# TensorE in the program's order through layer 1, W' made by pairs, and memory work one turn a step

## The chip, the cores and the metric

The kernel runs on one core of a Trainium2 chip. The metric is the device time of one execution in microseconds, as the median of several runs.

## The reference

Attention with a memory of 32 slots is followed by two MoE layers, each a product, a nonlinearity and a product. With B = 4, H = 8, S = 576, D = 64, M = 32 there are 2304 tokens of width 512; the hidden width is 2048.

```python
def _attn_ref(q, k, v, phi):            # per batch and head
    a = softmax(phi, over=s)
    k_m = einsum('bhsm,bhsd->bhmd', a, k)
    v_m = einsum('bhsm,bhsd->bhmd', a, v)
    attn = softmax(q @ k_m.T / sqrt(D), over=m)
    return attn @ v_m

def _moe_ref(x, w_in, w_out):
    h = np.maximum(x @ w_in, 0.0)
    return h * h @ w_out

def _moe2_ref(x, w_in, w_out):
    h = x @ w_in
    g = h * tanh(log1p(exp(h)))
    return g @ w_out
```

The output is `_moe2_ref(_moe_ref(attention))`.

## The kernel before

**Layer 1.** The product of the attention's `v_m` with `w_in` is made first, per batch and per page of 256 hidden columns. The result is W', called `wp` in the code: the first layer is then attention weights (128 rows: four heads times 32 slots, two groups of heads) times W'. `w_part` (line 580) makes one W' part (b, j) for batch b and page j: 8 small matmuls in the program, 16 in the trace, into a PSUM tile with the tag "bb" of two banks. `w_pair` (line 605) makes two, (b, j) and (b, j + 1), 16 in the program and 32 in the trace. In both, ScalarE (ACT) then casts the sum to the high half and VectorE (DVE) subtracts for the low half; in `w_pair` the two halves of the tile are taken one after the other, either at once or, by `w_out`, in the next step. There is one buffer of "bb", and three others use it: the scores (`psc`, line 536), the transposes of softmaxed phi (`pt`, line 464), and the W' parts. A block there waits until the block ahead has been read out.

**A step.** `a_tile` (line 724) runs over hidden blocks fc of 128. A step makes `h` by six matmuls for each segment of tokens (lines 713 to 715, the first product), then ACT applies relu and square, copies to `g` (line 742), and DVE subtracts for the low half of `g` (line 745). The second product, 12 matmuls of `a` from `g` (lines 665 to 667), is put LAG = 3 steps behind. `tick` starts weight work on ACT, DVE and the queues, `mid` a piece of the attention of a later batch, `post` the W' work. Banks of `h` are "mm" and "b0" in turns, or "mm" alone.

**The tiles.** `subs` holds four narrow tiles (b = 0, 1 and both halves of 288 tokens) for hidden blocks 0 to 3, then two passes of three wide tiles of 344, 464 (232 of batch 0 and 232 of batch 1) and 344 tokens, for blocks 4 to 9 and 10 to 15. Behind these come four narrow tiles, both halves of batch 2 and of batch 3, with all 16 blocks each, and then the second layer. Batches 2 and 3 get their memory products meanwhile: `kv_later` returns a generator of turns (`kv_unit`, line 515), `attn_later` one for scores and softmax; `run_step` takes so many turns a step. A turn of `kv_unit` uses "b0" for `pk` (the product of softmaxed phi with k and v) and `pkt` (its transpose), and loads phi, k and v of the next batch on SP's queue.

**The weights of layer 2** are folded at the same time: `raw_i` and `raw_o` are loaded on SP's queue, ACT and DVE make the sums and casts `st` in tiles that share space with the outputs `ys`, POOL's queue stores them, and layer 1's outputs are stored to `y` on SP's queue (line 698).

**What sets the order.** Instructions go through a list scheduler that arranges each engine's order by a simulated timeline; it may put a block of W' earlier or cut it. Within `written(...)` the engines named keep the program's order: the first tile on DVE and ACT, and the second layer on TensorE, DVE and ACT. Everything between was free before. Steps (fc) below are counted from 0 in each tile.

Of the kernel before, what the change touches and what calls it, by code (L numbers as in the profile page):

```python
# [8 lines left out]
F32R = mybir.dt.float32r  # L9
# [7 lines left out]
B, H, S, D, M = 4, 8, 576, 64, 32  # L17
DM, FF = 512, 2048
P = 128
# [21 lines left out]
def body(tc, q, kvm, kvt, phi, w_in1, w_out1, w_in2, w_out2, out):  # L41
# [21 lines left out]
    def page(shape, dt, name):  # L63
        return PG.tile(shape, dt, tag="pg", name=name, bufs=NPG)
# [8 lines left out]
    for p in range(2):  # L73
        t = Y.tile([P, (NC + 1) * P], F32, name=f"phi{p}")
# [62 lines left out]
    wt = {}  # L137
# [15 lines left out]
    @contextlib.contextmanager  # L153
    def written(*engines):

        traced = nc.cur_bb.bb.instructions
        last = {x.engine: x for x in traced}
        seen = traced[-1]
        yield
        start = next(k for k in reversed(range(len(traced))) if traced[k] is seen) + 1  # L160
        for x in traced[start:]:
            if x.engine not in engines:
                continue
            if x.engine in last:
                tc.add_manual_dep(
                    x, last[x.engine].name,
                    mybir.DependencyInfo(mybir.DependencyClass.NoSync, mybir.DependencyReason.DATA),
                    reason="written")
            last[x.engine] = x
# [265 lines left out]
    rc_t, et_t, kk_t, kT, vT = {}, {}, {}, {}, {}  # L435
# [142 lines left out]
    wp = {}  # L578

    def w_part(b, j, lo, hi, split=False):  # L580

        ps = banks2(f"pw{b}{j}{lo}")[:, :, :hi - lo]
        for g in range(4):
            for p in range(2):
                nc.tensor.matmul(  # L585
                    ps[M * g:M * g + M, p], vT[b][D * p:D * p + D, M * g:M * g + M],
                    wt["i1", j][D * p:D * p + D, g, lo:hi], start=True, stop=True)
        if (b, j) not in wp:
            wp[b, j] = page([P, 2, 2, 256], F32R, f"wp{b}{j}")
        t = wp[b, j]  # L590
        nc.scalar.copy(t[:, 0, :, lo:hi], ps)
        rest = lambda: nc.vector.tensor_sub(t[:, 1, :, lo:hi], ps, t[:, 0, :, lo:hi].bitcast(F32))
        if split:
            return rest
        rest()
# [6 lines left out]
                f()  # L602
        wait_w.clear()

    def w_pair(b, j, now=False):

        ps = banks2(f"pw{b}{j}p")
        for i in range(2):
            for g in range(4):
                for p in range(2):  # L610
                    nc.tensor.matmul(
                        ps[M * g:M * g + M, p, 256 * i:256 * i + 256],
                        vT[b][D * p:D * p + D, M * g:M * g + M],
                        wt["i1", j + i][D * p:D * p + D, g], start=True, stop=True)

        def take(i):
            t = wp[b, j + i] = page([P, 2, 2, 256], F32R, f"wp{b}{j + i}")
            nc.scalar.copy(t[:, 0], ps[:, :, 256 * i:256 * i + 256])
            nc.vector.tensor_sub(t[:, 1], ps[:, :, 256 * i:256 * i + 256], t[:, 0].bitcast(F32))

        for i in range(2):
            if now:
                take(i)
            else:
                wait_w.append(lambda i=i: take(i))
# [131 lines left out]
    bounds = [sum(GROUPS[:i]) for i in range(len(GROUPS) + 1)]  # L757
# [13 lines left out]
    def place(i):  # L771
        if i in deep:
# [3 lines left out]
    c1 = Conv(order, place,  # L776
              lambda key, u: key != "i1" or u < 8 or (1, u // 2 - 4) in wp)
# [244 lines left out]
    def kv_later(b):  # L1022
        def nxt(p):
            if p == 0 and b > 1:
                load_kv(b, 1)
            if b + 1 < B:
                load_phi(b + 1, p)
                if p == 1:
                    load_kv(b + 1, 0)
                    load_tail(b + 1)  # L1030
        u = lazy(lambda: kv_unit(b, "b0", nxt))

        return [[u, 3], [iter(range(2)), 2], [u, 4]] if b > 1 else [[u, 5]]

    def attn_later(b, half):
        def nxt():
            if b < 2:
                if (b, half) == (1, 0):
                    load_q(2, 0)
                return  # L1040
            nb, nh = (b, 1) if half == 0 else (b + 1, 0)
            if nb < B:
                load_q(nb, nh)
        return [[lazy(lambda: attn_unit(b, half, nxt)), 5 if b > 1 else 4]]
# [3 lines left out]
    subs = [(0, bounds[1], half_of(b, half)) for b in range(2) for half in range(2)]  # L1048
# [14 lines left out]
    lanes, n_steps = [], 1  # L1063
    for i, (f0, f1, segs) in enumerate(subs):
        b, half, part = i // 2, i % 2, (i - 4) % 3 if i > 3 else None
        final = i == len(subs) - 1
        if i == 0:
            with written(mybir.EngineType.DVE, mybir.EngineType.Activation):
                first_tile()
            c1.hold = False  # L1070
            c1.store()
            c1.load(2 * GROUPS[0] - 3)
            continue
        elif i == 1:
            c1.limit, c1.after, c1.paced = 2 * GROUPS[0], "lo", True
            lanes, n_steps = [[iter(range(2)), 2]] + attn_later(1, 1), 1
        elif i == 2:
            c1.limit, c1.after = len(c1.order), (1, 0)
        elif i == 3:
            drain(lanes)  # L1080
            c1.after = (1, 1)
            load_q(2, 0)
            load_phi(2, 0)
            load_phi(2, 1)
            load_kv(2, 0)
            load_tail(2)
        elif i == 4:
            c1.after = None
        elif i == len(subs) - 2:
            lanes, n_steps = kv_later(2), 2  # L1090
        elif final:
            drain(lanes)
            lanes, n_steps = attn_later(2, 0), 2
            load_page(0)
            load_page(1)

        def tick(fc):
            if len(c1.done) < 2 * NF:
                c1.tick()
            else:  # L1100
                if not fold.loaded:
                    fold.load(3)
                if part and fc - f0 in (0, LAG + 1):
                    fold.tags = (("x", "at"), ("ys0", "x", "at"), ("ys0",), ("ys0", "ys1"))[
                        2 * part - 2 + (fc > f0)]
                if final or part == 1 and fc > f0:
                    fold.tick(pops=1)

        def mid(fc):
            run_step(lanes, n_steps)  # L1110

        def post(fc):
            if part is None:
                if half == 0 and fc % 2 == 0 and fc + 2 < f1 and i != 2:
                    c1.need("i1", fc + 3)
                    w_part(b, fc // 2 + 1, 0, 256)
                if i == 1 and fc + 1 == f1:
                    w_part(1, fc // 2, 0, 256)
                if half == 1 and fc + 2 == f1:
                    if b == 0:  # L1120
                        w_part(1, f0 // 2, 0, 256)
                    else:
                        c1.need("i1", f1 + 1)
                        w_part(0, f1 // 2, 0, 256)
            elif part == 0:
                if (fc - f0) % 2 == 0 and fc + 2 < f1:
                    c1.need("i1", fc + 3)
                    w_part(0, fc // 2 + 1, 0, 256)
                if fc >= f0 + 2:
                    c1.need("o1", fc - 2)  # L1130
                if fc + 1 == f1:
                    c1.need("o1", fc)
                if fc + 2 == f1:
                    w_part(1, f0 // 2, 0, 256)
            elif part == 1:
                if fc == f0:
                    w_pair(1, f0 // 2 + 1, True)
            elif fc + 2 == f1 and not final:
                c1.need("i1", f1 + 1)
                w_part(0, f1 // 2, 0, 256)  # L1140
            if final and fc - f0 in (1, 3):
                w_pair(2, fc - f0 - 1)
            if final and fc < f1 - 2:
                load_page(fc - f0 + 2)

        a_tile(segs, f0, f1, tick, mid, post, ("mm",) if i in (0, 1, 5) else ("mm", "b0"))
# [8 lines left out]
        return f  # L1155

    b, nb = 2, 3
    lanes = [attn_later(b, 1), [[iter(range(2)), 2]] + kv_later(nb)]

    def mid(fc):  # L1160
        for lane in lanes:
# [13 lines left out]
    lanes = [attn_later(nb, 0) + attn_later(nb, 1)]  # L1175
# [136 lines left out]
    a_tile(half_of(B - 1, 0), 0, NF, tick3(0), nothing, post0, acc_tags)  # L1312
    a_tile(half_of(B - 1, 1), 0, NF, tick3(1), nothing, post1, acc_tags)
    assert not y0
    layer2 = written(mybir.EngineType.PE, mybir.EngineType.DVE, mybir.EngineType.Activation)
    layer2.__enter__()
    flush()
# [14 lines left out]
    now = 0  # L1332
# [139 lines left out]
    banks, tmp, g = {}, {}, {}  # L1472
# [4 lines left out]
    for now, (kind, i, one, two) in enumerate(plan):  # L1477
# [11 lines left out]
        if now + AHEAD < len(plan) and plan[now + AHEAD][0] == "b":  # L1489
            _, _, j, k = plan[now + AHEAD]  # L1490
# [73 lines left out]
```

## Time and profile before

| | us |
|---|---|
| median of 3 runs | 737.28 (735.41 to 737.71) |
| profiled execution | 734.3 |
| its span | 732.5 |
| TensorE busy | 725.0 (99%) |
| DVE busy | 523.5 (71%) |
| ACT busy | 414.0 (57%) |
| layer 1's second product, lines 665 to 667 | 140.2, 140.8 and 127.9 busy |
| layer 1's first product, lines 713 to 715 | 78.2, 75.8 and 75.8 busy |

The span is the time of the instructions on the core; the profiled execution's own time has 1.8 us around it. In a group "x464" counts instructions. Layer 1 from the first wide tile to the last narrow one takes about 60 to 400 us of the span.

### The profile page before, as it was taken

To read this page: it belongs to the slowest core of one execution; us is meant where nothing else is said; L and a number is where in the kernel's file an instruction comes from. 1 tells how busy PE (TensorE), PEld (TensorE's weight loads), DVE (VectorE), ACT (ScalarE), POOL (GpSimd) and SP (SyncE) were. 2 spreads that over 40 slices of the span, in tenths; PEclk is the share of its full clock that TensorE was granted. 3 is DMA by queue.
4 is the path that set the end of the run, shared out by engine and by line. 5 is a ranking of instruction groups with operands and counts; after the bars stand their busy time and mean duration, and the time that the engine had idled before them with its cause. 6 is when DMAs were issued, how large, how long until landed. Compare 5 with 4: busy or idle time off the path is not lost.

```text
span 732.5 us, 15173 instructions
## 1 busy us (share of the span) xinstructions
PE 725.0 (99%) x5417; PEld 691.5 (94%) x5417; DVE 523.5 (71%) x1142; ACT 414.0 (57%) x937; POOL 62.0 (8%) x120
## 2 busy tenths in 40 slices
PE   8999999999999999999999999999999999999998
PEld 7788988998888899999999999999999999999997
DVE  5999766343887889899957769854658873556674
ACT  4869757553766698767644347532336551335552
POOL 0000000000122333243311000000000000000000
PEclk9999999999999999999999999999999999999999
DMA  9997542044689899878969998899988899888882
GB/s 337 400 407 280 178 136 92 30 159 151 229 303 377 305 316 339 287 274 312 330 230 358 392 315 250 271 298 305 307 251 249 253 293 297 250 252 249 254 272 77
DMA packets 88011, 195.26 MB, mean 267 GB/s; under 512 B 10112, under 2 KB 21376, under 8 KB 87936
## 3 DMA queue, kind: packets, MB, share of 16 engines
q1 hardware_dynamic: 78976, 164.92, 67.7%
q0 software_dynamic: 8960, 29.37, 10.3%
q8 instruction: 43, 0.70, 0.4%
q14 instruction: 32, 0.26, 0.1%
HBM read 151.26 MB, written 42.99 MB: 265 GB/s over the span
## 4 chain that ended last, share of the span: by engine, by line
PE 91%; DMA 4%; DVE 2%; ACT 2%; issue 1%; SPq 0%; DVEq 0%; ACTq 0%
PE a L667 8%; PE a L665 8%; PE a L666 8%; PE hb L1361 8%; PE hb L1363 8%; PE hb L1362 8%; PE h L713 5%; PE h L714 4%; PE h L715 4%; DMA raw_i<-in_moe_w_in_dram 2%; PE pw L585 1%; PE fill L789 1%; PE b22acc L1447 1%; PE b12acc L1445 1%; PE b02acc L1447 1%; PE b22acc L1445 1%
## 5 line engine op out<-in xcount | busy, mean ns | idle before, releaser
L665 PE MATMUL a<-g,o1h 128*128 128x288 f32 (+2 forms) x464 | 140.2, 311 | 1.3 <-ACT g L742 1.3
L666 PE MATMUL a<-g,o1l 128*128 128x288 f32 (+2 forms) x464 | 140.8, 309 | 0.0
L667 PE MATMUL a<-g,o1h 128*128 128x288 f32 (+2 forms) x464 | 127.9, 310 | 0.0
L1361 PE MATMUL hb<-ych,u 128*128 128x384 f32 x336 | 113.2, 337 | 0.0
L1362 PE MATMUL hb<-ycl,u 128*128 128x384 f32 x336 | 113.1, 336 | 0.0
L1363 PE MATMUL hb<-ych,u 128*128 128x384 f32 x336 | 113.0, 336 | 0.0
L1368 ACT ACTIVATE a<-hs 128x384 f32<-128x384 f32 x72 | 37.8, 526 | 117.9 <-DVE hs L1372 117.9
L665 PEld LDWEIGHTS a<-g,o1h 128*128 128x128 f32 x464 | 86.8, 188 | 5.5 <-ACT g L742 1.8
L736 ACT ACTIVATE s<-h 128x288 f32<-128x288 f32 (+2 forms) x112 | 49.1, 438 | 72.3 <-PE h L715 70.4
L666 PEld LDWEIGHTS a<-g,o1l 128*128 128x128 f32 x464 | 87.3, 188 | 2.1 <-issue 1.3
L667 PEld LDWEIGHTS a<-g,o1h 128*128 128x128 f32 x464 | 82.4, 188 | 2.9 <-DVE st L393 0.5
L1411 ACT CAST oph<-a 128x384 fp32r<-128x384 f32 x120 | 59.4, 512 | 37.9 <-PE b22acc L1447 7.4
L1412 DVE TENSOR_TENSOR opl<-a,oph 128x384 fp32r<-128x384 f32 x120 | 63.0, 554 | 22.5 <-ACT oph L1411 15.9
L713 PE MATMUL h<-ah,wp 128*128 128x288 f32 (+2 forms) x256 | 78.2, 306 | 0.4
L714 PE MATMUL h<-al,wp 128*128 128x288 f32 (+2 forms) x256 | 75.8, 296 | 0.2 <-DVE al L575 0.2
L715 PE MATMUL h<-ah,wp 128*128 128x288 f32 (+2 forms) x256 | 75.8, 297 | 0.0
L745 DVE TENSOR_TENSOR g<-s,g 128x288 fp32r<-128x288 f32 (+2 forms) x112 | 54.0, 484 | 22.2 <-ACT g L742 21.7
L1361 PEld LDWEIGHTS hb<-ych,u 128*128 128x128 f32 x336 | 63.0, 188 | 0.3 <-DVE hu L1383 0.3
L1363 PEld LDWEIGHTS hb<-ych,u 128*128 128x128 f32 x336 | 63.0, 188 | 0.0
L1362 PEld LDWEIGHTS hb<-ycl,u 128*128 128x128 f32 x336 | 63.0, 188 | 0.0
L1372 DVE TENSOR_TENSOR hs<-hu,hb 128x384 f32<-128x384 f32 x72 | 39.7, 553 | 25.9 <-PE hb L1363 24.1
L713 PEld LDWEIGHTS h<-ah,wp 128*128 128x128 f32 x256 | 48.1, 188 | 9.4 <-issue 4.1
(322 smaller groups left out, 1529.0 us busy)
## 6 DMA issues: line engine op xcount, KB each, us to landing
u<-wf_i SPq DMA_DIRECT2D x168, 256.0 KB, 4.0
u<-wf_o SPq DMA_DIRECT2D x168, 256.0 KB, 3.2
raw_i<-in_moe_w_in_dram SPq DMA_DIRECT2D x32, 512.0 KB, 5.7
raw_o<-in_moe_w_out_dram SPq DMA_DIRECT2D x32, 512.0 KB, 6.3
wf_i<-st POOLq DMA_DIRECT2D x56, 256.0 KB, 5.2
wf_o<-st POOLq DMA_DIRECT2D x56, 256.0 KB, 4.9
win1r<-w_i SPq DMA_DIRECT2D x16, 512.0 KB, 5.3
kv<-in_kvm_dram SPq DMA_DIRECT2D x5, 1024.0 KB, 7.4
```

Source lines behind the costliest of these rows:

```text
L665: nc.tensor.matmul(o, wh[:, c, cs], sh, start=first, stop=False)
L666: nc.tensor.matmul(o, wl[:, c, cs], sh, start=False, stop=False)
L667: nc.tensor.matmul(o, wh[:, c, cs], sl, start=False, stop=last)
L713: nc.tensor.matmul(ph, w[:, 0, hg, fs], hi[:, hg], start=(hg == 0), stop=False)
L714: nc.tensor.matmul(ph, w[:, 0, hg, fs], lo[:, hg], start=False, stop=False)
L715: nc.tensor.matmul(ph, w[:, 1, hg, fs], hi[:, hg], start=False, stop=(hg == 1))
L745: marks["lo"] = nc.vector.tensor_sub(sl, s, sh.bitcast(F32))
L1361: nc.tensor.matmul(ps, wh, yh[:, d], start=(j < 4 and d == 0), stop=False, **kw)
L1362: nc.tensor.matmul(ps, wh, yl[:, d], start=False, stop=False, **kw)
L1363: nc.tensor.matmul(ps, wl, yh[:, d], start=False, stop=end, **kw)
L1411: marks["hi"] = nc.scalar.copy(hi, x)
L1412: marks["lo"] = sub(lo, x, hi.bitcast(F32))
```

## The change

Three things. From the first wide tile (i == 4) to the start of the second layer TensorE keeps the program's order (`layer1`), so no matmul of that stretch is moved ahead of another. The W' parts of these tiles are made by pairs: (0,3) with (0,4) and (0,6) with (0,7) at the first step of a pass's first tile, and, across batches, (0,5) with (1,5) two steps before the end of the first pass's last tile; (1,2) stays a single part. The pair (0,3), (0,4) needs page 4 of `w_in` two steps earlier than the single part did. Last, the third batch's memory work (`kv_later(2)`) starts at i == 7 after five idle steps and takes one turn a step; before, it started at i == 8 and took two. The fourth batch's starts after three idle steps, where there were two.

```diff
--- before.py
+++ after.py
@@ -602,19 +602,20 @@
                 f()
         wait_w.clear()
 
-    def w_pair(b, j, now=False):
+    def w_pair(b, j, now=False, across=False):
 
         ps = banks2(f"pw{b}{j}p")
-        for i in range(2):
+        two = [(b, j), (b + 1, j) if across else (b, j + 1)]
+        for i, (bb, jj) in enumerate(two):
             for g in range(4):
                 for p in range(2):
                     nc.tensor.matmul(
                         ps[M * g:M * g + M, p, 256 * i:256 * i + 256],
-                        vT[b][D * p:D * p + D, M * g:M * g + M],
-                        wt["i1", j + i][D * p:D * p + D, g], start=True, stop=True)
+                        vT[bb][D * p:D * p + D, M * g:M * g + M],
+                        wt["i1", jj][D * p:D * p + D, g], start=True, stop=True)
 
         def take(i):
-            t = wp[b, j + i] = page([P, 2, 2, 256], F32R, f"wp{b}{j + i}")
+            t = wp[two[i]] = page([P, 2, 2, 256], F32R, "wp%d%d" % two[i])
             nc.scalar.copy(t[:, 0], ps[:, :, 256 * i:256 * i + 256])
             nc.vector.tensor_sub(t[:, 1], ps[:, :, 256 * i:256 * i + 256], t[:, 0].bitcast(F32))
 
@@ -1030,7 +1031,7 @@
                     load_tail(b + 1)
         u = lazy(lambda: kv_unit(b, "b0", nxt))
 
-        return [[u, 3], [iter(range(2)), 2], [u, 4]] if b > 1 else [[u, 5]]
+        return [[u, 3], [iter(range(2)), 2], [u, 4]] if b > 2 else [[u, 7]]
 
     def attn_later(b, half):
         def nxt():
@@ -1086,8 +1087,10 @@
             load_tail(2)
         elif i == 4:
             c1.after = None
-        elif i == len(subs) - 2:
-            lanes, n_steps = kv_later(2), 2
+            layer1 = written(mybir.EngineType.PE)
+            layer1.__enter__()
+        elif i == len(subs) - 3:
+            lanes, n_steps = [[iter(range(5)), 5]] + kv_later(2), 1
         elif final:
             drain(lanes)
             lanes, n_steps = attn_later(2, 0), 2
@@ -1123,21 +1126,21 @@
                         c1.need("i1", f1 + 1)
                         w_part(0, f1 // 2, 0, 256)
             elif part == 0:
-                if (fc - f0) % 2 == 0 and fc + 2 < f1:
-                    c1.need("i1", fc + 3)
-                    w_part(0, fc // 2 + 1, 0, 256)
+                if fc == f0:
+                    c1.need("i1", fc + 5)
+                    w_pair(0, fc // 2 + 1, True)
                 if fc >= f0 + 2:
                     c1.need("o1", fc - 2)
                 if fc + 1 == f1:
                     c1.need("o1", fc)
-                if fc + 2 == f1:
+                if fc + 2 == f1 and f0 == bounds[1]:
                     w_part(1, f0 // 2, 0, 256)
             elif part == 1:
                 if fc == f0:
                     w_pair(1, f0 // 2 + 1, True)
             elif fc + 2 == f1 and not final:
                 c1.need("i1", f1 + 1)
-                w_part(0, f1 // 2, 0, 256)
+                w_pair(0, f1 // 2, True, True)
             if final and fc - f0 in (1, 3):
                 w_pair(2, fc - f0 - 1)
             if final and fc < f1 - 2:
@@ -1155,7 +1158,7 @@
         return f
 
     b, nb = 2, 3
-    lanes = [attn_later(b, 1), [[iter(range(2)), 2]] + kv_later(nb)]
+    lanes = [attn_later(b, 1), [[iter(range(3)), 3]] + kv_later(nb)]
 
     def mid(fc):
         for lane in lanes:
@@ -1312,6 +1315,7 @@
     a_tile(half_of(B - 1, 0), 0, NF, tick3(0), nothing, post0, acc_tags)
     a_tile(half_of(B - 1, 1), 0, NF, tick3(1), nothing, post1, acc_tags)
     assert not y0
+    layer1.__exit__(None, None, None)
     layer2 = written(mybir.EngineType.PE, mybir.EngineType.DVE, mybir.EngineType.Activation)
     layer2.__enter__()
     flush()
```

Three places show what the order does. The rows are TensorE's. In the first, `pw24p` is the pair (2,4) and (2,5), at the start of the third batch's first half, `pt` the transposes of phi for the fourth batch, `h` a first product (tile, step), `a` a second product with the step of its `g`. Before:

```order
L666 MATMUL a_0_0_0_2650<-g_0_1_2724,o1l_418 128x288
L611 MATMUL pw24p<-win1r_2530,vT_2310 32x256 x8
L611 MATMUL pw24p<-win1r_2578,vT_2310 32x256 x8
L713 MATMUL h_0_3_2807<-ah_2504,wp_2499 128x288
...
L715 MATMUL h_0_5_2926<-ah_2504,wp_2599 128x288
L464 MATMUL pt_2842<-ident,phi_79 128x128 x5
L667 MATMUL a_0_0_0_2650<-g_0_3_2825,o1h_642 128x288
```

and now:

```order
L668 MATMUL a_232_10_3_2365<-g_232_15_2632,o1h_1749 128x344
L612 MATMUL pw24p<-win1r_2527,vT_2344 32x256 x8
L612 MATMUL pw24p<-win1r_2575,vT_2344 32x256 x8
L714 MATMUL h_0_3_2800<-ah_2501,wp_2496 128x288
...
L666 MATMUL a_0_0_0_2647<-g_0_0_2670,o1h_417 128x288
...
L714 MATMUL h_0_4_2848<-ah_2501,wp_2596 128x288
...
L716 MATMUL h_0_4_2848<-ah_2501,wp_2596 128x288
L464 MATMUL pt_2879<-ident,phi_79 128x128 x5
L666 MATMUL a_0_0_0_2647<-g_0_1_2721,o1h_417 128x288
```

The pair stands behind the wide tile's last second product, and the transposes follow it by two first products and one second product; before, three first products and the second products between them stood there.

The second place is the pair (3,0) and (3,1), `pw30p`, and the scores of the fourth batch, `psc`. Before, in the third batch's first half:

```order
L667 MATMUL a_0_0_3_2653<-g_0_11_3232,o1h_1493 128x288
L611 MATMUL pw30p<-win1r_3384,vT_3194 32x256 x4
L713 MATMUL h_0_13_3281<-ah_2504,wp_3009 128x288
...
L611 MATMUL pw30p<-win1r_3384,vT_3194 32x256 x4
L611 MATMUL pw30p<-win1r_3386,vT_3194 32x256 x3
L665 MATMUL a_0_0_0_2650<-g_0_12_3266,o1h_1645 128x288
...
L611 MATMUL pw30p<-win1r_3386,vT_3194 32x256 x4
L713 MATMUL h_0_14_3313<-ah_2504,wp_3012 128x288
...
L611 MATMUL pw30p<-win1r_3386,vT_3194 32x256
```

and now, in the second half:

```order
L668 MATMUL a_288_0_3_3392<-g_288_0_3409,o1h_417 128x288
L612 MATMUL pw30p<-win1r_3381,vT_3230 32x256 x8
L612 MATMUL pw30p<-win1r_3383,vT_3230 32x256 x8
L714 MATMUL h_288_4_3581<-ah_2501,wp_2596 128x288
...
L666 MATMUL a_288_0_0_3389<-g_288_1_3462,o1h_417 128x288
...
L714 MATMUL h_288_5_3627<-ah_2501,wp_2596 128x288
...
L716 MATMUL h_288_5_3627<-ah_2501,wp_2596 128x288
L536 MATMUL psc_3650<-q_3421,kT_3228 32x288 x4
L536 MATMUL psc_3650<-q_3423,kT_3228 32x288 x4
```

The pair is whole, and the scores follow it by two steps; before it was cut into four pieces in the tile ahead.

The third is the third batch's first memory product, `pk`, in the last wide pass. Before:

```order
L715 MATMUL h_344_11_2115<-ah_683,wp_2015 128x232
L665 MATMUL a_0_10_0_1839<-g_0_14_1991,o1h_1775 128x344
...
L665 MATMUL a_0_10_1_1840<-g_0_14_1991,o1h_1775 128x344
L611 MATMUL pw16p<-win_6_1497,vT_650 32x256 x8
L611 MATMUL pw16p<-win_7_1649,vT_650 32x256 x8
L488 MATMUL pk_2134<-kv_979,et_2072 32x128 x16
L488 MATMUL pk_2134<-kt_981,et_2072 32x128 x4
L666 MATMUL a_0_10_1_1840<-g_0_14_1991,o1l_1776 128x344
```

and now:

```order
L668 MATMUL a_0_10_3_1858<-g_0_13_1975,o1h_1615 128x344
L612 MATMUL pw16p<-win_6_1465,vT_650 32x256 x8
L612 MATMUL pw16p<-win_7_1619,vT_650 32x256 x8
L714 MATMUL h_344_11_2112<-ah_342,wp_1818 128x232
...
L716 MATMUL h_344_11_2112<-ah_683,wp_1821 128x232
L488 MATMUL pk_2131<-kv_979,et_2069 32x128 x16
L488 MATMUL pk_2131<-kt_981,et_2069 32x128 x4
L666 MATMUL a_0_10_0_1855<-g_0_14_2000,o1h_1749 128x344
```

`pk` no longer stands beside the W' pair (1,6), (1,7) but directly behind a first product.

## Rows read from the trace of the kernel before

**Rows 1.** Page, part 2: busy tenths, granted clock and DMA share in 40 slices

```profile
PE   8999999999999999999999999999999999999998
PEclk9999999999999999999999999999999999999999
DMA  9997542044689899878969998899988899888882
```

**Rows 2.** Page, part 4: the chain that ended last, shares by engine

```profile
PE 91%; DMA 4%; DVE 2%; ACT 2%; issue 1%; SPq 0%; DVEq 0%; ACTq 0%
```

**Rows 3.** TensorE's timeline, single block and pair: start us, us, line, operation, [idle before]

```profile
64.83 0.29 PE L715 MATMUL h<-ah,wp 128*128 128x288 f32 x1
65.06 0.66 PE L585 MATMUL pw<-win,vT 64*32 64x256 f32 x16
65.65 0.79 PE L667 MATMUL a<-g,o1h 128*128 128x288 f32 x4
...
209.78 0.30 PE L665 MATMUL a<-g,o1h 128*128 128x288 f32 x1
209.91 0.29 PE L666 MATMUL a<-g,o1l 128*128 128x288 f32 x1
210.13 1.09 PE L611 MATMUL pw24p<-win1r,vT 64*32 64x256 f32 x32
211.16 0.40 PE L713 MATMUL h<-ah,wp 128*128 128x288 f32 x1
211.39 0.29 PE L714 MATMUL h<-al,wp 128*128 128x288 f32 x1
```

**Rows 4.** TensorE's timeline: blocks that were cut

```profile
108.84 0.63 PE L585 MATMUL pw<-win,vT 64*32 64x256 f32 x6
...
179.97 0.68 PE L536 MATMUL psc<-q,kT 64*32 64x288 f32 x4
...
246.52 0.64 PE L611 MATMUL pw30p<-win1r,vT 64*32 64x256 f32 x8
...
252.00 0.62 PE L611 MATMUL pw30p<-win1r,vT 64*32 64x256 f32 x2
```

**Rows 5.** TensorE's timeline: two gaps ahead of second products

```profile
216.83 0.30 PE L667 MATMUL a<-g,o1h 128*128 128x288 f32 x1
217.58 0.40 PE L665 MATMUL a<-g,o1h 128*128 128x288 f32 x1 [0.45 <-ACT g L742]
...
236.97 0.29 PE L715 MATMUL h<-ah,wp 128*128 128x288 f32 x1
238.12 0.40 PE L665 MATMUL a<-g,o1h 128*128 128x288 f32 x1 [0.85 <-ACT g L742]
```

**Rows 6.** ACT's timeline: casts of W' pair (2,4), waits, a relu

```profile
212.72 0.41 ACT L392 CAST st<-ct_i 128x256 fp32r<-128x256 f32 x1 [0.65 <-DMA y<-ys]
...
213.33 0.58 ACT L618 CAST wp<-pw24p 128x512 fp32r<-128x512 f32 x1
...
215.48 0.41 ACT L392 CAST st<-ct_i 128x256 fp32r<-128x256 f32 x1 [0.69 <-DMA y<-ys]
...
216.61 0.58 ACT L618 CAST wp<-pw24p 128x512 fp32r<-128x512 f32 x1
...
236.00 0.67 ACT L339 ACTIVATE raw_i<-raw_i 128x512 f32<-128x512 f32 x1 [2.08 <-DMA raw_i<-in_moe_w_in_dram]
...
263.44 0.42 ACT L736 ACTIVATE s<-h 128x288 f32<-128x288 f32 x1
```

**Rows 7.** DVE's timeline: subtraction of the second half of two pairs

```profile
217.78 0.65 DVE L619 TENSOR_TENSOR wp<-pw24p,wp 128x512 fp32r<-128x512 f32 x1
...
267.90 0.69 DVE L619 TENSOR_TENSOR wp<-pw30p,wp 128x512 fp32r<-128x512 f32 x1
```

**Rows 8.** SP's queue: stores of y issued in the third batch's first steps

```profile
208.71 2.67 SPq L698 DMA_DIRECT2D y<-ys  x4
```

**Rows 9.** Groups by line, shapes apart: relu on ACT, wide tile

```profile
L736 ACT ACTIVATE s<-h 128x464 f32<-128x464 f32 x12 | 6.7, 559 | 24.0 <-PE h L715 24.0
```

## Prediction

> **What bounds the kernel now.** Read the page's slices first [rows 1]: TensorE is busy eight to nine tenths in the first slice and nine or more in all others but the last, and the clock that it was granted is the higher level, 2.4 GHz, throughout. The chain that ended last [rows 2] is 91% TensorE. So almost any time that TensorE spends or saves between the first wide tile and the second layer is the kernel's; a copy on ScalarE (ACT) or VectorE (DVE) counts only where TensorE stands still for it. What is left to look for in TensorE's own timeline is of two kinds: blocks of small matmuls, which cost more than their rows, and gaps in which a matmul waited. Rows 3 and 4 show the first kind, rows 5 the second. A page's busy share hides both: during a block the engine is called busy.
>
> **What a block costs.** Matmuls of 288 columns start 0.13 us apart (209.78 to 209.91) [rows 3]. Around a W' block of 16 matmuls the starts are 64.83 and 65.65, 0.82 apart; less the one pitch, the block holds the path for 0.69. The matmul behind a block takes another 0.10 (211.16 to 211.39 is 0.23). So a single block is 0.79 us. A pair of 32 matmuls goes from 209.91 to 211.16: 1.25 less 0.13 plus 0.10, or 1.22. The cost hardly depends on how many matmuls are in a block below 16: by their rows 16 took 0.66 us [rows 3], 6 took 0.63, 8 took 0.64, 2 took 0.62 and 4 of the scores 0.68 [rows 4]. Cutting a block in two costs a whole block more; putting two into a pair saves 0.36.
>
> **What the change gives.** (a) Six W' parts become three pairs: (0,3) with (0,4), (0,5) with (1,5), (0,6) with (0,7). Before, (0,5) and (1,5) were cut in two by the scheduler (6 and 10 matmuls; the piece at 108.84 stands for the four), so there were 4 whole blocks and 4 pieces, 8 x 0.79 = 6.3; now 3 x 1.22 = 3.7. Gain 2.6. (b) The scores cut in two (4 at 179.97 [rows 4], 12 a step later) stand together: 0.8. (c) pw30p, four pieces from 246.52 to 252.00 [rows 4]: 4 x (0.66 + 0.10) = 3.0 becomes 1.2. Gain 1.8. (d) Two pairs that stood directly beside a memory product (pk) now stand apart from it: one more restart and drain each, 0.3 lost. Together 4.9 gained, and these terms are safe, since the order is now fixed and prints whole blocks.
> (e) Two gaps of before: 216.83 to 217.58 (0.75 - 0.13 + 0.10 = 0.72) and 236.97 to 238.12 (1.15 - 0.13 + 0.10 = 1.12) [rows 5]. In both an `a` matmul waited for the cast of `g` of a step that had gone by only just before: the scheduler had let the second products catch up with the first. In the program's order they come three steps behind the relu, so ACT's stop of 2.08 us for a weight load before 236.00 [rows 6] no longer reaches them. Gain 1.8. Sum of the gains: 6.7 us.
>
> **What the change costs.** The scheduler had moved TensorE's blocks to where their bank was free; the program's order takes that away. W' pairs, scores and transposes of phi (pt) share one PSUM tile ("bb", two banks, one buffer), so a block can't start before both copies of the pair ahead (an ACT cast and a DVE subtraction for each half) are done, and now nothing steps past it.
> Before, the pair pw24p started at 210.13, ACT cast its halves at 213.33 and 216.61, and DVE ended the second at 217.78 + 0.65 = 218.43 [rows 3, 6 and 7]: 8.3 us after the start. The pt block stood behind all that, and nobody noticed. In the order of after only one first product (6 x 0.13), one second product (12 x 0.13) and one first product stand between: 1.22 + 0.8 + 1.6 + 0.8 = 4.4 us. With the eviction as before TensorE stands 3.9 us. It won't be quite as before: ACT's two waits there (0.65 before 212.72, 0.69 before 215.48) are for stores of y, which SP issued from 208.71 on [rows 6 and 8], before the pair; in the new order the wide tile's last sums end right ahead of the pair, so the stores leave about 2 us later against it. Following ACT's and DVE's queues of the changed program with these durations I get 4.8 (bounds 1.1, if the second cast followed the first directly: 8.3 less 3.28 plus 0.48 is 5.5; and 5.4). Relu of the next step stands behind those casts, but the second products are three steps back, so TensorE loses nothing else there.
> The second place is pw30p and the scores two steps on, again 4.4 us apart, where before the order put the pair into the tile ahead, many steps from the scores. From the relu of a step to the end of DVE's last subtraction there took 263.44 to 267.90 + 0.69, 5.15 us [rows 6 and 7]; that relu now starts 1.22 + 0.8 + 0.2 after the pair's start, so the end comes at about 7.4, a stall of up to 2.9; down the queue of after it is 2.1. I take 2.1 (bounds 0, if the two casts come together; and 3.5).
> Third, the third batch's memory work now begins a tile earlier with a turn each step. It moves nothing on the path but two blocks, a pk and a pkt, which use the bank "b0" and now directly follow the first product that wrote b0: they wait for its relu, 0.56 us for 464 columns [rows 9], plus the signal: 0.6 each, 1.2 (bounds 0.6 and 1.6). The loads that its turns issue on SP move with it to a place where the DMA engines are half idle (the page's slices at 120 to 180 us [rows 1]); I cost them at nothing.
> Small waits: the first product that uses (0,3) comes 0.4 after its pair can be cast; pw22p is closer behind pw20p (0.3); a first product behind the raw load on ACT [rows 6] 0.75. 1.5 together, bounds 0 and 5 (the load of 2.08 us has no slack to be absorbed in if it is hit twice).
> Stalls: 4.8 + 2.1 + 1.2 + 1.5 = 9.6 us, and by the bounds 1.7 to 15.5.
>
> A rule of the Trainium skill bears on this. In the trace a waiting matmul is followed by nothing until it starts, as between 236.97 and 238.12 [rows 5]. The skill ("TensorE: Matmul & The Clock Gate", Part 3, "The mechanism") says why: matmuls keep strictly to their order, only weight loads are pulled ahead. That speaks against a fixed order: whatever is late holds all that is behind. The trace agrees, and the sum above already goes by it.
>
> **Rivals.** *Faster (the other side).* The evictions are prompt: with the order fixed, the pairs' casts are put where ACT has just done a relu, and the y stores land before they are wanted. Then pw24p costs 1.1, pw30p nothing, the pk blocks 0.6, the rest 0.5: stalls 2.2, net -4.5, 732.8 us. It decides where both stalls together fall under some 4 us. For it: in rows 6 ACT's two waits for y alone are 1.3 us of the 8.3. Against it: the casts of the two halves stay a step apart in the order of ACT.
> *No change.* ACT's two waits for y go, with nothing in their place (8.3 - 1.3 = 7.0, stall 2.6), pw30p 1.5, pk 1.2, the rest 1.5: 6.8 against 6.7, 737.4 us.
> *Worse.* Upper bounds everywhere: 15.5 - 6.7 = 8.8 us, 746 us. In the third batch's first half all first products share one bank ("mm"), so that every delay of ACT holds the next product too, and ACT's wait for a raw load [rows 6] could then cost its full 2.08 more than once. It also holds a clock: the granted clock of rows 1 stays high over gaps of 1 us [rows 5], and no row has a gap of 4 us. If the clock fell to 1.2 GHz behind one, the next 12 matmuls would take 3.2 instead of 1.6 us. The skill (same page, Part 1, "What's actually happening") has an idle TensorE go back to that level; no run here shows it.
>
> **How the numbers follow.** The profiled execution took 734.3 us, the median of the runs is 737.28; sums are differences made on the first, and are put on the median. Forecast: 9.6 - 6.7 = +2.9, so 737.2 by the profile and 740.2 us by the median; its own range is 738.5 to 743.5. Chances: forecast 0.40, faster 0.25, no change 0.25, worse 0.10. A change within 0.3% (2.2 us) can't be told from none with this kernel's runs. With the edges of each case: faster 0.26, same 0.27, slower 0.47. The range holds 8 in 10 from 732.5 to 745.0: half of the faster case and most of the worse one lie within or at its ends.
>
> **What will show it.** Right: TensorE's timeline has W' blocks of 32 and no pieces; no gap at the `a` matmuls named in rows 5; one gap of 4 to 5 us ahead of pt in the third batch's first half and one near 2 ahead of the scores in its second, both released by DVE's `wp` subtraction; gaps of 0.6 ahead of two kv blocks. Wrong: if these gaps are absent, or if gaps appear at the first products (released by a relu) in the stretch from 200 to 260 us, or if the granted clock falls below the higher level. The gains (a) to (c) are wrong if a pair block holds the path longer than 1.25 us.

## The result, and the profile after

The changed kernel takes 740.04 us (median, 738.81 to 741.4), the kernel before in the same measurement 735.72 (733.79 to 737.71). The ratio is 1.0057, with a 95% interval of 1.004 to 1.0074: slower by 0.6%, or 4.2 us. The forecast was 740.2 us and +2.9 us. That the absolute time agrees within 0.2 us is luck: the kernel before came out 1.6 us lower than the 737.28 that the forecast started from, and the change cost 1.3 us more than forecast.

In the profiled execution the span is 737.0 us, where it was 732.5. All of it lies ahead of the second layer. TensorE's first `hb` matmul of that layer came at 376.66 us before and comes 4.5 us later now, and from there to the end both take 355.8. The rows are of TensorE's timeline (start, duration), before and then after:

```profile
376.66 0.34 PE L1361 MATMUL hb<-ych,u 128*128 128x384 f32 x1
```

```profile
381.15 0.34 PE L1365 MATMUL hb<-ych,u 128*128 128x384 f32 x1
```

The page's chain of after is to be read against [rows 2]: 91% TensorE has become 88%, and DVE's 2% has become 5%.

```profile
PE 88%; DVE 5%; ACT 3%; DMA 2%; issue 2%; POOL 0%; DVEq 0%; ACTq 0%; POOLq 0%
```

Where TensorE stood between 60 and 400 us is told by the view of its waits. Before, that view has two waits of a second product for the cast of `g` [rows 5]; after, both are gone, and these stand there (total, times, longest):

```profile
engine line waited for: us in total, times, longest us
PE pt L464 <- DVE wp L620: 3.8, 1, 3.8
PE psc L536 <- issue: 1.9, 1, 1.9
PE h L714 <- DVE wp L620: 1.4, 1, 1.4
PE pkt L503 <- ACT s L737: 0.6, 1, 0.6
PE pk L488 <- ACT s L737: 0.6, 1, 0.6
PE a L666 <- DVE ys L692: 0.2, 1, 0.2
```

The largest is the one ahead of the transposes. TensorE's timeline after, at the same place as the pair in [rows 3]:

```profile
208.43 0.32 PE L668 MATMUL a<-g,o1h 128*128 128x344 f32 x1
208.68 1.09 PE L612 MATMUL pw24p<-win1r,vT 64*32 64x256 f32 x32
209.71 0.40 PE L714 MATMUL h<-ah,wp 128*128 128x288 f32 x1
...
212.86 0.29 PE L716 MATMUL h<-ah,wp 128*128 128x288 f32 x1
216.94 1.30 PE L464 MATMUL pt<-ident,phi 128*128 128x128 f32 x5 [3.79 <-DVE wp L620]
217.89 0.59 PE L666 MATMUL a<-g,o1h 128*128 128x288 f32 x1
218.27 0.44 PE L667 MATMUL a<-g,o1l 128*128 128x288 f32 x1
218.51 0.44 PE L668 MATMUL a<-g,o1h 128*128 128x288 f32 x1
...
219.69 0.30 PE L667 MATMUL a<-g,o1l 128*128 128x288 f32 x1
```

The pair is whole and holds the path for 1.12 us as before (208.43 to 209.71 less the pitch of 0.16). Then come six, twelve and six matmuls at 0.13, and the transposes start 4.08 us behind the last of them. Look next at the starts behind: 218.27, 218.51 and so on are 0.24 apart, not 0.13, until 219.69. The granted clock shows it, in a table by stretches (stretch, length, busy time of each engine, clock, DMA share, GB/s):

```profile
core 0: us, PE busy (x) PEld busy (x) DVE busy (x) ACT busy (x) POOL busy (x), PEclk, DMA share, GB/s
212.90:216.90 4.00, 0.25 (x2) 0.02 (x1) 3.21 (x8) 3.31 (x9) 1.05 (x2) 0.92 1.04 391
216.90:219.60 2.70, 2.66 (x12) 2.69 (x13) 2.70 (x8) 1.83 (x5) 1.74 (x3) 0.50 0.96 378
219.60:222.00 2.40, 2.40 (x41) 2.23 (x43) 1.20 (x3) 0.41 (x1) 0.54 (x1) 0.99 0.88 217
266.00:268.30 2.30, 0.42 (x4) 0.18 (x2) 2.07 (x4) 2.30 (x7) 1.07 (x2) 1.00 0.99 390
```

Behind the gap the clock is 0.50, the lower level of 1.2 GHz, for 2.7 us. In the gap ahead of the scores (266.0 to 268.3) it stays at 1.00, and behind it the matmuls start 0.13 apart (269.24 and 269.37 below). The page's row of granted clock in 40 slices doesn't show such a stretch: it has a 9 in every slice here too, as in [rows 1]. What held the transposes is in the queues of ACT and DVE, to be read against [rows 6 and 7]:

```profile
211.23 0.40 ACT L737 ACTIVATE s<-h 128x288 f32<-128x288 f32 x1
211.53 0.58 ACT L619 CAST wp<-pw24p 128x512 fp32r<-128x512 f32 x1
...
213.37 0.42 ACT L392 CAST st<-raw_i 128x256 fp32r<-128x256 f32 x1 [0.67 <-DMA y<-ys]
...
214.93 0.57 ACT L619 CAST wp<-pw24p 128x512 fp32r<-128x512 f32 x1
```

```profile
216.10 0.69 DVE L620 TENSOR_TENSOR wp<-pw24p,wp 128x512 fp32r<-128x512 f32 x1
```

The first cast of the pair has the relu of its step ahead of it. Ahead of the second (214.93) stand the prelu of a weight load, a cast that waited 0.67 us for a store of y, a square and two casts; DVE's subtraction for it ends at 216.79, 8.1 us behind the pair's start. It was 8.3 before. The eviction didn't get slower; the transposes have come nearer.

The other places, from TensorE's timeline:

```profile
155.04 0.27 PE L716 MATMUL h<-ah,wp 128*128 128x232 f32 x1
155.95 1.08 PE L488 MATMUL pk<-kv,et 128*32 128x128 f32 x32 [0.65 <-ACT s L737]
...
174.26 0.44 PE L503 MATMUL pkt<-ident,kk 128*128 128x128 f32 x2 [0.65 <-ACT s L737]
...
268.35 0.72 PE L536 MATMUL psc<-q,kT 64*32 64x288 f32 x16 [1.93 <-issue]
...
269.24 0.29 PE L667 MATMUL a<-g,o1l 128*128 128x288 f32 x1
269.37 0.29 PE L668 MATMUL a<-g,o1h 128*128 128x288 f32 x1
...
302.91 0.30 PE L668 MATMUL a<-g,o1h 128*128 128x288 f32 x1
304.59 0.37 PE L714 MATMUL h<-ah,wp 128*128 128x288 f32 x1 [1.38 <-DVE wp L620]
```

The scores start 2.23 us behind the start of the product ahead of them (266.12), which is 2.0 over the usual distance, and 0.1 after DVE ends the pair pw30p (267.56 + 0.69). The trace names no releaser there ("issue"); that it is this subtraction follows from the times and from the shared space. The row at 304.59 is a place that the prediction does not have.

### The profile page after: what moved, and what is told of

It reads as the page before. It is cut to its first block, busy times and chain, and to the rows that moved or that the text cites. A ratio compares the mean times of both kernels' runs of the same rounds, so it can differ in the third digit from the quotient of the medians.

```text
span 737.0 us, 15174 instructions
## 1 busy us (share of the span) xinstructions
PE 722.1 (98%) x5417; PEld 692.7 (94%) x5417; DVE 525.4 (71%) x1142; ACT 415.5 (56%) x937; POOL 62.0 (8%) x120
## 4 chain that ended last, share of the span: by engine, by line
PE 88%; DVE 5%; ACT 3%; DMA 2%; issue 2%; POOL 0%; DVEq 0%; ACTq 0%; POOLq 0%
PE hb L1365 8%; PE hb L1366 8%; PE hb L1367 8%; PE a L666 8%; PE a L668 8%; PE a L667 8%; PE h L714 4%; PE h L715 4%; PE h L716 4%; PE pk L488 1%; DMA wf_i<-st 1%; PE fill L790 1%; PE b22acc L1449 1%; PE b12acc L1451 1%; PE b22acc L1451 1%
## 5 line engine op out<-in xcount | busy, mean ns | idle before, releaser
L666 PE MATMUL a<-g,o1h 128*128 128x288 f32 (+2 forms) x464 | 144.0, 314 | 0.2 <-DVE ys L692 0.2
L667 PE MATMUL a<-g,o1l 128*128 128x288 f32 (+2 forms) x464 | 142.4, 308 | 0.0
L668 PE MATMUL a<-g,o1h 128*128 128x288 f32 (+2 forms) x464 | 140.5, 309 | 0.0
L666 PEld LDWEIGHTS a<-g,o1h 128*128 128x128 f32 x464 | 87.3, 189 | 5.4 <-issue 3.5
L668 PEld LDWEIGHTS a<-g,o1h 128*128 128x128 f32 x464 | 86.6, 189 | 1.2
```

The lines of the kernel that those rows point to most:

```text
L666: nc.tensor.matmul(o, wh[:, c, cs], sh, start=first, stop=False)
L667: nc.tensor.matmul(o, wl[:, c, cs], sh, start=False, stop=False)
L668: nc.tensor.matmul(o, wh[:, c, cs], sl, start=False, stop=last)
```

## The experiments

Times are medians; each ratio is to the kernel before, measured beside it on the same chip.

**The order alone, and the pairs alone.** The first kernel adds the fixed order to the kernel before, and nothing else; the second takes it out of the changed kernel.

```diff
         elif i == 4:
             c1.after = None
+            layer1 = written(mybir.EngineType.PE)
+            layer1.__enter__()
...
+    layer1.__exit__(None, None, None)
     layer2 = written(mybir.EngineType.PE, mybir.EngineType.DVE, mybir.EngineType.Activation)
```

> The kernel before with TensorE's order fixed from the first wide tile on, and nothing else: single W' parts, memory work at two turns a step. Theory (the order gives whole blocks and keeps the second products three steps back, and pays in waits for the shared PSUM tile bb): gains of about 4.4 us (scores and pw30p whole, the two gaps of before gone), costs as in the changed kernel (about 11) plus more: the transposes come one step earlier behind pw24p (gap of about 7 us in place of 4) and one memory product directly behind its transposes (1 to 2 us). Net about +9 us, 744 to 746 us beside 736 of before. Rival (the order is neutral, the pairs and the turns cost the 4 us): about the time of before, 735 to 737 us.

Measured: 744.67 us, ratio 1.0124 (1.0111 to 1.0137). Three of TensorE's waits in it:

```profile
PE pt L464 <- DVE wp L619: 6.2, 1, 6.2
PE psc L536 <- issue: 1.9, 1, 1.9
PE pk L488 <- ACT et L467: 1.2, 1, 1.2
```

The transposes come one step earlier behind pw24p, and the wait is 6.2 us in place of 3.8. The memory product that stands directly behind its own transposes waits 1.2 for ACT's copy. Both sizes are near those expected (about 7, and 1 to 2).

> The changed kernel without the fixed order: W' by pairs and memory work a turn a step, and the scheduler free on TensorE. Theory: the pairs' gain is mostly given back, since the scheduler cuts pw03p, pw05p, pw24p, pw30p and a block of scores again, and there are no waits of some us for bb: within 1.5 us of before, 734.5 to 737 us. Rival (pairs and turns cost): about 740 us, as the changed kernel.

Measured: 736.01 us, ratio 1.0008 (0.9999 to 1.0017). So pairs and turns alone change nothing that can be measured, and the slowdown needs the fixed order. In the trace the free scheduler has cut blocks again: pw03p and pw24p stand in two pieces, pw05p and pw30p in three.

**The pairs and the turns, undone one at a time** under the fixed order:

```diff
-                if fc == f0:
-                    c1.need("i1", fc + 5)
-                    w_pair(0, fc // 2 + 1, True)
+                if (fc - f0) % 2 == 0 and fc + 2 < f1:
+                    c1.need("i1", fc + 3)
+                    w_part(0, fc // 2 + 1, 0, 256)
...
-                w_pair(0, f1 // 2, True, True)
+                w_part(0, f1 // 2, 0, 256)
```

> The changed kernel with single W' parts in the two wide passes, whole because the order is fixed, in place of the three new pairs. Theory: six single blocks of 0.79 us in place of three pairs of 1.22: 1.1 us slower by the blocks, plus at most 1 us where a single part waits for the one two steps ahead: 741 to 742 us. Rival (the pairs need a page earlier or hold the shared tile longer): the same as or faster than the changed kernel, 739 to 740 us.

Measured: 743.89 us, ratio 1.0117 (1.0103 to 1.0131), 0.6% above the changed kernel's and more than expected. The blocks are as priced: between 62 us and the first transposes (153.34 here, 150.15 in the changed kernel) this kernel loses 1.0 us. What was not expected is the clock: in this profile the stretches at the lower level are longer, one behind the transposes and one, which the changed kernel's profile doesn't have, behind the scores:

```profile
220.00:225.00 5.00, 4.88 (x21) 4.91 (x22) 3.98 (x10) 1.81 (x5) 2.28 (x4) 0.50 0.90 288
273.40:277.00 3.60, 3.60 (x23) 3.52 (x16) 3.47 (x9) 0.88 (x3) 0.54 (x1) 0.53 1.00 338
```

Matmuls of 288 columns start 0.24 apart in them; counted against 0.13 they cost 3.5 us in this execution and 0.8 in the changed kernel's. It isn't this one execution alone: the granted clock of the whole span is 0.992 to 0.995 in all four runs here, and 0.994 to 0.998 in the changed kernel's six. So the pairs are worth about 1 us by their blocks, and most of the rest of the difference goes with the clock, by these counts; why it stayed low for longer here isn't shown.

```diff
-        return ... if b > 2 else [[u, 7]]
+        return ... if b > 1 else [[u, 5]]
...
-        elif i == len(subs) - 3:
-            lanes, n_steps = [[iter(range(5)), 5]] + kv_later(2), 1
+        elif i == len(subs) - 2:
+            lanes, n_steps = kv_later(2), 2
```

> The changed kernel with the third batch's memory work as it was: from i == 8 on, two turns a step. Theory: with the order fixed, two turns a step put the second memory product directly behind its own transposes, which ACT must first copy: a gap of 1.5 to 2 us there, and one or two of the 0.7 to 0.9 waits for b0 go or stay: 0 to 2 us slower than the changed kernel, 740 to 742 us. Rival (the earlier memory work costs, by its loads or its ACT work): faster than the changed kernel, 738 to 739 us.

Measured: 741.68 us, ratio 1.0085 (1.007 to 1.0101), at the expected place: the same wait of 1.2 us for `et` as with the order alone, and the pkt's wait for b0 gone. Two more things are longer in its profile and take part in the difference: the wait of the first product that stands at 304.59 in the changed kernel is 2.0 us in place of 1.4, and matmuls at the lower clock cost some 2.9 us in place of 0.8. So what the turns alone are worth isn't separated.

**Moving the waits away.** First the transposes alone:

```diff
-    lanes = [attn_later(b, 1), [[iter(range(3)), 3]] + kv_later(nb)]
+    lanes = [attn_later(b, 1), [[iter(range(7)), 7]] + kv_later(nb)]
```

> The changed kernel with the fourth batch's memory work four steps later (seven idle steps, where there were three), so that its first transposes come six blocks of first and second products behind the pair ahead and not three. Theory: the gap of 4.1 us ahead of the transposes goes, and with it the stretch at the lower clock behind it (some 0.8 us): 4.5 to 5 us less than the changed kernel, about 735.2 us, with granted clock 1.00 from 210 to 222 us. Rival (the stores of y and the raw loads hold ACT, and the next matmul that needs ACT waits in any case): the gap moves to a first or second product or to pw26p, at most 1.5 us gained.

Measured: 738.76 us, ratio 1.004 (1.0027 to 1.0053): a gain of some 1.3 us, hardly more than the noise and far from the 4.5 of the theory, and so the rival's. TensorE's gaps in the stretch are now ahead of first products, released by a relu:

```profile
216.91 0.40 PE L714 MATMUL h<-ah,wp 128*128 128x288 f32 x1 [1.12 <-ACT s L737]
...
223.41 0.40 PE L714 MATMUL h<-ah,wp 128*128 128x288 f32 x1 [0.24 <-ACT s L737]
...
226.71 0.40 PE L714 MATMUL h<-ah,wp 128*128 128x288 f32 x1 [0.65 <-ACT s L737]
```

The 4 us had covered these. Then four waits at once: the transposes, the scores one step later, the last pair (3,6) a step earlier, and the third batch's first pk and its pkt in the bank that the step doesn't use.

```diff
-    lanes = [attn_later(nb, 0) + attn_later(nb, 1)]
+    lanes = [attn_later(nb, 0) + [[iter(range(1)), 1]] + attn_later(nb, 1)]
...
-        if fc % 4 == 3:
-            w_pair(nb, fc // 2 - 1)
+        if fc in (3, 7, 11, 14):
+            w_pair(nb, min(6, fc // 2 - 1))
...
-            kv_mem(b, p, (0, 1), tag)
+            kv_mem(b, p, (0, 1), "mm" if (b, p) == (2, 0) else tag)
...
-        kv_heads(b, (0, 1), tag)
+        kv_heads(b, (0, 1), "mm" if b == 2 else tag)
```

> The changed kernel with four waits moved away: the fourth batch's memory work four steps later, its second scores one step later, the last W' pair (3,6) a step earlier, and two blocks of the third batch's memory work in the bank mm in place of b0. Theory: the gaps of the changed kernel (4.1 us plus the lower clock 0.8; 2.0; 1.55; 0.7 and 0.9) go, together about 10 us, and the gains of the order stay: 730 to 731.5 us, about 5 us (0.7%) faster than before. Rival (other work on ACT or DVE ends last, and the waits come back elsewhere): 735 to 738 us.

Measured: 733.83 us, ratio 0.9982 (0.997 to 0.9993): between the two. The four gaps are gone but for 0.3 us ahead of the transposes; those ahead of first products stay, 3.2 us together. ACT's timeline of this kernel shows why:

```profile
214.82 0.40 ACT L737 ACTIVATE s<-h 128x288 f32<-128x288 f32 x1
...
217.22 0.41 ACT L392 CAST st<-ct_i 128x256 fp32r<-128x256 f32 x1 [1.71 <-DMA y<-ys]
217.53 0.44 ACT L738 ACTIVATE s<-s 128x288 f32<-128x288 f32 x1
```

A relu of the third batch is done at 215.2; its square stands behind a cast that waits 1.71 us for a store of y. Relu of the next step is behind that, and in this tile the next first product needs the one bank "mm" that this relu empties.

**Two banks, or no stores of y.** Two banks for that tile (`("mm", "b0")`, the memory products in the bank not in use):

> The kernel with the four waits moved away, and in the third batch's first half two banks for the first product (mm and b0 in turns) in place of mm alone, with each memory product in the bank that the step doesn't use. Theory (with one bank each first product waits for the relu of the step ahead, which stands on ACT behind casts that wait for stores of y): the four gaps there (1.28, 0.57, 0.63 and 0.74 us between 213 and 226 us) go, about 3 us: 730.5 to 731.5 us, 0.6% faster than before. Rival (ACT is late by itself in that stretch, so the wait moves to the second products or the W' blocks): at most 1 us gained, 733 us.

Measured: 734.6 us, ratio 0.9991 (0.9982 to 1.0): the rival's. The first products no longer wait, and TensorE is the sooner at the transposes:

```profile
222.55 0.29 PE L716 MATMUL h<-ah,wp 128*128 128x288 f32 x1
226.08 0.74 PE L464 MATMUL pt<-ident,phi 128*128 128x128 f32 x5 [3.23 <-DVE wp L620]
```

A second bank doesn't make ACT earlier, it only moves the place where TensorE meets it. The longer gap also brought the lower clock back: 0.997 or 0.998 over the span in ten of these eleven runs, 0.999 or 1.000 in eight of the ten with one bank. So the stores were taken out of ACT's way, in the changed kernel and with nothing else:

```diff
-            tags = [f"ys{j}" for j in range(4) if not (j == 3 - 3 * half and fc <= LAG or ...
+            tags = [f"ys{j}" for j in range(4) if not (
+                j > 1 and half == 0 and fc <= LAG + 3 or j == 3 - 3 * half and fc <= LAG or ...
```

> The changed kernel, with the casts of weights kept out of the space of the two outputs that are being stored in the first seven steps of the third batch's first half, so that no cast on ACT waits there for a store of y. Theory as forecast (the casts of the pair stand in ACT's queue behind other work; the stores lengthen that by 1 to 1.5 us): the gap ahead of the transposes goes from 4.1 to about 2.6 us, the kernel to about 738.5. Rival (the stores are the whole cause): the gap falls under 1 us and the kernel to 736 or less.

Measured: 736.02 us, ratio 1.0014 (1.0 to 1.0027). The gap ahead of the transposes is 2.16 us in place of 4.08:

```profile
213.74 0.29 PE L716 MATMUL h<-ah,wp 128*128 128x288 f32 x1
215.90 0.74 PE L464 MATMUL pt<-ident,phi 128*128 128x128 f32 x5 [1.87 <-DVE wp L620]
```

The stores are half of that gap, not the whole; the other half is the nearness. The kernel gained some 3.2 us by the ratios, more than expected. In the profile the first product that waited 1.55 us at 304.59 waits 0.6, and the gap ahead of the scores is 0.35 shorter; that goes a part of the way. The clock goes a part of it too. In the profiled execution it was low for 3.5 us, behind a gap of half the length:

```profile
216.60:220.10 3.50, 3.50 (x18) 3.50 (x17) 1.59 (x4) 1.10 (x3) 0.54 (x1) 0.52 1.01 347
```

But of this kernel's ten runs five have a granted clock of 1.000 over the span, and they take 735.2 to 735.7 us; the other five have 0.997 or 0.998 and take 736.4 to 737.4. The two groups are some 1.4 us apart, which is about what the starts 0.24 apart add up to in the profile. Only every second execution has the stretch, where all six of the changed kernel are below 1.000.

Then both together, the four waits moved and the stores out of the way; and the same with two banks and the transposes one more step later (with one idle turn fewer behind them).

> The kernel with the four waits moved away (one bank for the first product), with the casts of weights also kept out of the outputs being stored, as in the run without places of y. Theory: the gaps ahead of first products between 213 and 226 us (1.28, 0.57, 0.63, 0.74) were ACT's waits for stores of y; they fall under 1 us together and the transposes wait less than 0.5 us: 731 to 732 us, 0.5% faster than before. Rival (ACT is late there by the number of its instructions, as the run with two banks suggests, where the wait moved to the transposes): the gaps stay or move, 733 to 735 us.

Measured: 730.57 us, ratio 0.9929 (0.9913 to 0.9946), the fastest kernel here. The stretch from 213 to 227 us in the table by stretches, first with the four waits moved alone, then with the stores out of the way too:

```profile
213.00:227.00 14.00, 11.19 (x101) 9.50 (x100) 10.94 (x25) 10.46 (x28) 4.77 (x9) 1.00 0.96 342
```

```profile
213.00:227.00 14.00, 14.00 (x160) 12.81 (x158) 11.27 (x28) 11.48 (x32) 4.86 (x10) 1.00 1.03 391
```

TensorE was busy 11.19 of 14 us, and now all 14. The clock is 1.000 over the span in all six runs.

> The kernel with two banks in the third batch's first half, with the casts kept out of the outputs being stored, and the fourth batch's first transposes one more step later (nine steps into the tile). Theory: the gap of 3.4 us ahead of these transposes, to which the wait moved with two banks, goes (2.4 us by the step, the rest by the stores): 730.5 to 731.5 us, 0.6% faster than before. Rival (the wait moves on again, to the next block that ACT must release): 733 to 735 us.

Measured: 731.11 us, ratio 0.9935 (0.9919 to 0.9951): the same. With ACT no longer late, neither the second bank nor the later step has anything to give.

**What of it is the order.** The fastest kernel with TensorE free again, and the kernel before with nothing but the stores out of ACT's way:

> The kernel with the four waits moved and the casts kept out of the outputs being stored, but with TensorE's order free again. Theory (the 5 us that this kernel is faster than before are the fixed order's whole blocks, which the free scheduler cuts again): pw03p in 2, (1,2) in 2, pw05p in 3, scores in 2, pw24p in 2, pk in 2 and 2, pw30p in 3 pieces, nine blocks more at 0.76 us, so 6 us slower than with the order fixed: 735 to 737 us, as before. Rival (the moved work and the free places give the gain, with any order): 731 to 732 us.

Measured: 737.88 us, ratio 1.002 (1.0006 to 1.0035), by the ratios 0.9% or 6.7 us above the same kernel with the order fixed. The blocks are cut again; pw30p stands in three:

```profile
259.32 0.66 PE L612 MATMUL pw30p<-win1r,vT 64*32 64x256 f32 x14
263.02 0.65 PE L612 MATMUL pw30p<-win1r,vT 64*32 64x256 f32 x12
264.59 0.63 PE L612 MATMUL pw30p<-win1r,vT 64*32 64x256 f32 x6
```

Its profiled execution is the slowest of eleven (741.74 us), so its waits may not be typical: a memory product there waits 2.0 us for a load of kv, and second products 1.7 us for DVE. So not all of the 6.7 is blocks, and how much is isn't separated.

> The kernel before with nothing but the casts kept out of the outputs being stored. Theory: before, these waits on ACT cost at most the gap of 0.7 us at 217 us, and the scheduler cuts pw30p in five now: within 1 us of before, 734.5 to 736.5 us. Rival (the stores of y were a cost in their own right): 2 us or more faster than before.

Measured: 734.76 us, ratio 0.9991 (0.9978 to 1.0004): no difference. In these kernels the stores cost only where a fixed order puts something behind them.

## Why the prediction was right, point by point

**The gains, 6.7.** The blocks are whole and a pair holds the path for 1.12 us plus 0.10, as priced; both gaps of [rows 5] are gone. Between 62 us and the last pair TensorE has 22 blocks of W' before and 14 after, as forecast. The end of layer 1 moved by +4.5 and the waits below come to 10.6, so the gains were some 6.1 in that execution; this is a difference, with the small deviations of all other matmuls in it. Free and fixed order in the last kernels differ by 6.7, of which the free one's waits are a part.

**The transposes, 4.8.** Forecast was the gap, and it was 4.0 over the usual distance of 0.13, with the lower clock behind it 5.2: about 0.5 for the transposes themselves and 0.8 for the matmuls behind. So the place was right, and the size was right by luck, through two errors that made up for each other. The walk down ACT's queue was 0.8 too long (the eviction took 8.1 us, so the 3.9 of "as before" was nearer than the 4.8), and the clock, held to be a small part of the rival *worse*, was left out of the sum. It was a part of the likeliest case, and the prediction's own sign of being wrong, a granted clock below the higher level, came true.

**The scores, 2.1.** 2.0. **The blocks on b0, 1.2.** 0.7 and 0.8 over the usual distance, so 1.5, near the upper bound. **Small waits, 1.5.** None of the three named is in this profile: the first product behind (0,3), pw22p and the one behind the raw load did not wait. In their place a second product waited for DVE's `ys`, 0.35 over the usual distance.

**What failed.** Not in the sum was the first product at 304.59, 1.55 us: its bank lies in the space of "bb", which the last pair pw36p still holds. The prediction followed only the blocks that share "bb", and not the banks that take its place. Before, DVE had read out pw36p by 300.10 (299.42 + 0.68), and no matmul waited for it. The sum of the waits came to 10.6 in place of 9.6 (5.2, 2.0, 1.5, 0.35 and 1.55), the net to +4.5 in the profile and +4.2 by the ratio, where +2.9 was forecast.

**The rivals.** *Faster* said that the evictions would be prompt; the second cast of pw24p came 3.4 us behind the first, as before (3.3). *Worse* had its mechanism right, the one bank behind ACT's waits for stores, but it showed only when the transposes were moved out of the way: at first the longer gap hid it. The Trainium skill's rule from the prediction, that matmuls keep their order ("TensorE: Matmul & The Clock Gate", Part 3, "The mechanism"), agrees with the trace at the largest gap: the second product behind the transposes reads a `g` that DVE had finished by 211.24 (210.79 + 0.45), and it starts at 217.89 only, behind them.

## What to carry to other kernels

Small matmul blocks cost by the block, so an order that keeps them whole is worth several us; but a fixed order must also be given the distance that a free one found, from each block to the read-out of the one ahead in the same PSUM space. Measure that distance in the trace of before (here 8 us behind a pair where ACT's queue is full), and put the next user that far away. It differs from place to place: in the fastest kernel the scores stand 6.8 us behind pw30p and don't wait, and 4.4 us behind it they waited 2.0. If one wait is removed, look for the one that it covered: here the engine behind it (ACT, held by stores) had to be freed as well, and only both together gave 0.7%.

## What was not expected of the hardware

The lower clock doesn't go by the length of the gap alone. Behind the gap of 4.1 us ahead of the transposes it lasted 2.7 us in the changed kernel and some 5 with single parts. Behind the gap of 2.2 us ahead of the scores it stayed at 1.00 in the changed kernel and fell to 0.53 with single parts. Without the stores of y it fell to 0.52 behind another gap of 2.2 us in the profiled execution, and five of ten executions of that same program have 1.000 over the whole span. In the rows such stretches cost 0.8 to 3.5 us in one execution.

The Trainium skill ("TensorE: Matmul & The Clock Gate", Part 1, "What's actually happening") has the clock fall after idle time and says, for the start of a kernel, that the point at which it rises varies from run to run. The rows here agree that it falls behind idle time, which no run had shown when the prediction was made; how long it stays low behind equal gaps differs in them.
